# Clustered attention with a top-2 mixture of experts on one core: the gate's products in 16 columns, a changed order around the first expert, less scratch for dynamic transfers

## The chip, the cores and the metric

One Trainium2 chip, one core of it. The metric is the device time of one execution in microseconds (us): the median of 3 runs. The five engines are named as in the profile: PE (matmuls, PEld its weight loads), DVE (vector), ACT (scalar), POOL (GpSimd), SP (the engine whose queue issues most transfers).

## What is computed

The reference, cut to what matters:

```python
# attention: q, k, v of shape (4, 8, 768, 64); 16 centroids for each head
q_assign = argmax(normalized q @ normalized centroids)     # k_assign likewise
mask = q_assign[:, :, :, None] == k_assign[:, :, None, :]
scores = where(mask, q @ k.T / 8, -1e9)
x = softmax(scores) @ v                                    # then (3072, 512): heads side by side
# mixture of experts: 8 experts, 512 -> 1024 -> 512
noisy = x @ w_gate + log1p(exp(x @ w_noise)) * noise
top2 = the two largest of 8;  weight = softmax of the two
out[token] = sum over its two experts of weight * (relu(x @ w1[e]) @ w2[e])
```

## The kernel before, in words

Four batches of 8 heads are worked off as 16 pairs of heads (p = 0 to 15; pairs 0 to 3 are batch 0, and so on). The attention is one list of 192 steps t, six key blocks for each of two heads of a pair; a step's `scores` (4 matmuls of 384 columns, two exponentials on ACT into `pe`), `split_p` of the step before (the low half `pl = pe - high half`, on POOL, for the last 19 steps on DVE) and `values` of the step four before (18 matmuls into `av`). In between stand helpers, put at a step (in thirds of a step) by the table `AT` and the method `at`: each engine gets its instructions in this order and works them off in order. The helpers that matter here:

- `load_qk` (L379): q and k of four heads of a batch, 4 x 768 x 64 floats each, on SP's queue. `a_split` transposes them on PE and writes `hl` (high and low halves, L463 on ACT and L464 on DVE, one buffer). `b_place` (L528) copies `hl` by ten transfers of SP into the score operands A and B. `b_mask` places the cluster masks `mk` into A. `b_max` (L557 on PE, L559 on DVE) finds the row maxima, `b_neg` and `b_negT` (L566 to L575) turn them and place them in B through `nm` and `nt`.
- At the end of a head `values` writes x: `rs` (L628, L629) from `av` and a factor `ch`, then `xt` (L631). `x_scale` makes a batch's factor in seven steps, the last of which, `heads` (L430), makes `ch` on DVE.
- `x_halves` (L667 on ACT, L668 on POOL) splits a pair's 128 columns of x into two f16 halves `xh`; `store_x` stores them, `turn_h` (L1136) transposes them by a transfer of SP into `xhT` (one buffer). `g_logits` (L686 to L695) multiplies them with the gate's weights: for each of 6 token blocks and both halves of x one matmul with 32 columns (high and low halves of 16 weights); DVE scales and adds up over the four pairs of a batch in `glg` (L690, L692), and after the fourth adds the two halves to `gl` (L695). `g_gate` is a chain of some 40 small instructions on DVE and ACT from `gl` to each token's two places in the experts' lists; `g_list` (L847, L848) writes them to a table by indirect transfers of POOL.
- Around the end: `load_list(0)` reads the first expert's list, `gather_x` (L1157, POOL) gathers four tiles of 128 tokens, `turn_x` (L1168, SP) transposes them into `xT`.

`experts` then runs, for the first expert, `layer1` over 8 blocks f of 128 hidden units for the first 512 tokens of its list (12 matmuls of 512 columns in each, then ACT and DVE write `hT`, L1186 and L1187), with w2's conversion (`split_w2`) in between, and the last batch's gate: `g_logits(15)` before block 3 (`ahead=3`), then the chain `fs` cut into pieces before the blocks. `l_hot` and `l_sum` (L821, L838) make the rest of the lists by matmuls, between the first tiles of `layer2`. The other seven experts follow the same way with 404-column matmuls.

Of the kernel before, what the change touches and what calls it, by code (L numbers as in the profile page):

```python
# [9 lines left out]
F32 = mybir.dt.float32  # L10
# [15 lines left out]
AT = dict(  # L26
    ahead=3,
    first={'place': -2.333, 'sims': [-3.333, -2.667], 'sum': [-2.333, -2.333], 'max1': -2.333, 'ge': -2.333, 'max2': -2.333, 'eq': -1.333, 'mask': -1.0, 'bmask': -1.0, 'ky': -2.333, 'split': [-5.333, -5.0, -5.333, -4.0], 'bmax': [3.667, 22.667], 'bstep': [1.0, 0.667], 'neg': [9.0, 26.667], 'negT': [9.333, 27.333]},
    L=4, qk=-20.667, v=-8.667,
    vscale=-0.667, vsplit=10.667, vstep=1.0, split=[-4.667, -3.667, -4.0, -3.333], place=-0.667,  # L30
    sims=[-3.0, 2.0], sum=[2.333, 3.333], max1=3.333, ge=3.667, max2=4.333, eq=4.667, mask=6.333, bmask=6.333,
    bmax=9.333, neg=20.333, negT=22.0, zero=31.0, zstep=12.0, zlist=21.0, v1=4.0, store=2.667, turn=6.667, glog=12.0,
    xh=1.333, xh0=4.0, list=[32.0, 32.0, 19.0], lstep=[2.0, 2.0, 1.1667], bstep=1.0,
    gate=[13.0, 13.0, 5.667], am=5.333, amstep=0.333, xs=6.0, ky=4.0, cut=[13, 20], gplace=[27.0, 27.0, 14.333],
    vd=[1, 1, 2, 3, 4, 5], sec=-6.0, qf=-4.0, place1=4.333,
    fv=[{'v': -5.0, 'vscale': 13.0, 'am': 24.333, 'amstep': 0.333, 'vsplit': 25.333, 'vstep': 2.0},
# [8 lines left out]
class Kernel:  # L45
# [175 lines left out]
    def attention(self, ctx):  # L221
# [17 lines left out]
        self.qk, self.vt, self.vv, self.am, self.xt, self.gx = {}, {}, {}, {}, {}, {}  # L239
        self.vm, self.ch, self.wm0 = {}, {}, {}  # L240
        self.ws = {(0, m): self.gp.tile([128, 2], F32, name=f"ws{m}") for m in (1, 2)}
        L = AT["L"]
# [11 lines left out]
        for p in range(NP):  # L254
            b, hp = divmod(p, H // 2)
            w = 12 * (p - 2)
            if hp == 0:
                for g in range(2):
                    at(w + T["qk"] + 24 * g + (T["qf"] if (b, g) == (0, 1) else 0), self.load_qk, b, g)
                    v = w + 24 * g  # L260
                    V = T["fv"][g] if p == 0 else T
                    at(v + V["v"] + (T["v1"] if (b, g) == (1, 0) else 0), self.load_v, b, g)
                    for h in range(0, 4, 2):
                        at(v + V["vscale"] + V["amstep"] * h, self.v_max, b, g, h)
                    chain(v + V["am"], V["amstep"], self.v_scale(b, g))
                    if g:
                        chain(v + V["xs"] - (4 if b else 0), 1.0 if b else 0.333, self.x_scale(b))
                    for h in range(4):
                        at(v + V["vsplit"] + V["vstep"] * h, self.v_split, b, g, h)
# [30 lines left out]
            if p + 1 < NP:  # L300
                at(z + T["xh"] + (T["xh0"] if p == 0 else 0), self.x_halves, p)
                at(z + T["store"] + (T["xh0"] if p == 0 else 0), self.store_x, p)
                turn, glog = (T["store"], 5.667) if p == NP - H // 2 - 1 else (T["turn"], T["glog"]) if p < NP - 2 else (5.0, 8.0)
                at(z + turn, self.turn_h, p)
                at(z + glog, self.g_logits, p)
            if hp == H // 2 - 1:
# [41 lines left out]
        for t in range(min(sched)[0], z + L + 2):  # L348
            u = t - L
            slot = lambda i: [f(*a) for f, a in sched.pop((t, i), [])]  # L350
            slot(0)
            if 0 <= t < z:
                self.scores(t // 12, (t % 12) // 6, t % 6)
            if 0 <= t - 1 < z:
                self.split_p((t - 1) // 12, ((t - 1) % 12) // 6, (t - 1) % 6)
            slot(1)
            if 0 <= u < z:
                p, s, kc = u // 12, (u % 12) // 6, u % 6
                for i in range(NJ):
                    if AT["vd"][i] == kc:  # L360
                        self.values(p, s, i)
            slot(2)
# [61 lines left out]
    def x_scale(self, b):  # L424
        nc = self.nc

        def heads():
            self.ch[b] = self.wk.tile([128, 8], F32, name="ch")
            for g in range(2):
                nc.vector.tensor_scalar(self.ch[b][:, 4 * g:4 * g + 4], self.am[b, g][:, 2, :], self.xsc[:, b, 0:1], None,  # L430
                                        op0=OP.mult)

        return self.power(self.wk, lambda: self.vm[b], lambda: self.xsc[:, b], 3) + [heads]
# [228 lines left out]
    def x_halves(self, p):  # L662
# [4 lines left out]
        nc.scalar.activation(xh[:, :, 0], x, AF.Copy)  # L667
        nc.gpsimd.tensor_tensor(xh[:, :, 1], x, xh[:, :, 0], op=OP.subtract)  # L668

# [6 lines left out]
    def g_logits(self, p):  # L676

        nc, NJ, E = self.nc, self.NJ, self.E
        b, hp = divmod(p, self.H // 2)
        s = self.wgs[:, 2:3]  # L680
        if hp == 0:
            self.lg = self.gp.tile([128, NJ, 2, 2 * E], F32, name="glg", bufs=1)
        t = self.ps()[:, :NJ * 4 * E].rearrange("p (j i e) -> p j i e", j=NJ, i=2)
        for j in range(NJ):
            for i in range(2):
                nc.tensor.matmul(t[:, j], self.xhT[:, 2 * j + i], self.wgh[:, hp], start=(j == 0 and i == 0),  # L686
                                 stop=bool(i), skip_group_check=True)
        if hp == 0:
            nc.vector.tensor_tensor(s, self.wgs[:, 0:1], self.xsc[:, b, 0:1], op=OP.mult)
            nc.vector.tensor_scalar(self.lg, t, s, None, op0=OP.mult)  # L690
        else:
            nc.vector.scalar_tensor_tensor(self.lg, t, s, self.lg, op0=OP.mult, op1=OP.add)  # L692
        if hp == self.H // 2 - 1:
            self.gl = self.gp.tile([128, NJ, 2 * E], F32, name="gl", bufs=1)
            nc.vector.tensor_tensor(self.gl, self.lg[:, :, 0], self.lg[:, :, 1], op=OP.add)  # L695

    def g_gate(self, b):
# [9 lines left out]
        def begin():  # L707
# [6 lines left out]
            T["p"] = self.aux  # L714
            nc.scalar.activation(w(0), self.gl[:, :, E:], AF.Abs)

# [9 lines left out]
        pt = lambda: T["p"][:, c0:c0 + NE + E]  # L726
        nl = lambda: self.gl[:, :, :E]
        ns = lambda: self.gl[:, :, E:]
        rf = lambda: T["rec"].bitcast(F32)
# [168 lines left out]
    def experts(self, ctx):  # L898
# [36 lines left out]
        self.unscale(0, self.lst0.bitcast(F32)[:, :, 1])  # L935
# [198 lines left out]
    def turn_h(self, p):  # L1134
        self.xhT = self.gp.tile([128, 2 * self.NJ, 128], F16, name="xhT", bufs=1)
        self.nc.sync.dma_start_transpose(self.xhT, self.xh.rearrange("p j i c -> p (j i c)"))  # L1136

# [140 lines left out]
```

## Time and profile before

| | |
|---|---|
| median of 3 runs | 1054.55 us (1050.92 to 1058.95) |
| profiled execution | 1046.11 us; span 1044.3 us |
| mean granted clock of PE over the span | 0.979 |
| PE busy | 976.2 us (93%) |
| DVE, POOL, ACT busy | 683.2, 569.6, 447.0 us |

The profile is of one execution. Busy time is the union of an engine's instructions; a row of a timeline gives start, duration and, in brackets, how long the engine was idle before and what released it.

### The profile page before, as it was taken

How to read it: one execution, taken by the hardware profiler on the slowest of the kernel's cores; microseconds unless marked ns; L12 is line 12 of the kernel's file. 1: busy time of each engine (PE TensorE's matmuls, PEld its weight loads, DVE VectorE, ACT ScalarE, POOL GpSimd, SP SyncE). 2: the span in 40 equal slices, each digit the busy share in tenths (PEclk: the TensorE clock that was granted, in tenths of full speed). 3: DMA queues.
4: the chain of work that ended last, by engine and by line, in shares of the span. 5: the costliest groups of instructions: out<-in, count | busy, mean ns of one | idle time of the engine just before them, and what ended most of it. 6: DMA issues, size and time to landing. Idle time of an engine off the chain costs nothing.

```text
span 1044.3 us, 21670 instructions
## 1 busy us (share of the span) xinstructions
PE 976.2 (93%) x8359; PEld 663.1 (63%) x8359; DVE 683.2 (65%) x1493; ACT 447.0 (43%) x875; POOL 569.6 (55%) x618
## 2 busy tenths in 40 slices
PE   5799899999989998987999999999999999999994
PEld 4578798889888897875455545445454454554541
DVE  5888678887889878895746555464564644646521
ACT  3467576758566767664122313124122241121400
POOL 9269596868997799974355225133251342522211
PEclk8899999999999999998999999999999999999997
DMA  7866888887988776746267565545656456663200
GB/s 202 213 166 140 204 202 220 219 209 172 216 202 213 169 180 139 199 108 149 97 162 224 147 190 173 136 144 149 167 177 159 133 158 152 182 154 131 61 34 35
DMA packets 181902, 169.34 MB, mean 162 GB/s; under 512 B 93159, under 2 KB 159079, under 8 KB 181794
## 3 DMA queue, kind: packets, MB, share of 16 engines
q1 hardware_dynamic: 167990, 131.02, 50.7%
q0 software_dynamic: 13296, 36.38, 11.1%
q8 instruction: 67, 1.10, 0.4%
q10 hardware_dynamic: 508, 0.50, 0.3%
q14 instruction: 41, 0.34, 0.1%
HBM read 81.80 MB, written 26.12 MB: 103 GB/s over the span
## 4 chain that ended last, share of the span: by engine, by line
PE 42%; issue 7%; DVE 2%; POOL 2%; DMA 1%; SPq 0%; ACT 0%; POOLq 0%; DVEq 0%
PE ring L1177 20%; PE ring L1217 19%; POOL out L1230 1%; PE ring L1207 1%; POOL xt L1192 1%; DMA xg<-xs,lst 1%; DVE wm L1101 1%; PE ring L1211 0%; SPq L1168 0%; DMA xhT<-xh 0%; DVE hT L1187 0%; PE ring L838 0%; DVE w2t L1113 0%; DMA out<-yo,idx 0%; PE ring L166 0%
## 5 line engine op out<-in xcount | busy, mean ns | idle before, releaser
L599 POOL TENSOR_TENSOR pl<-pe 128x768 f16<-128x768 f32 x173 | 251.8, 1470 | 58.3 <-ACT pe L588 54.6
L1177 PE MATMUL ring<-xT,w1t 128*128 128x404 f16 (+2 forms) x1536 | 266.9, 334 | 0.0
L1217 PE MATMUL ring<-w2t,hT 128*128 128x512 f16 x1152 | 250.8, 379 | 0.4 <-DVE w2t L1113 0.4
L588 ACT ACTIVATE pe<-ring,l 128x384 f32<-128x384 f32 x384 | 201.4, 577 | 83.2 <-PE ring L587 73.2
L559 DVE TENSOR_REDUCE mm<-ring 128x1 f32<-128x384 f32 x384 | 193.1, 548 | 51.3 <-PE ring L557 50.9
L1177 PEld LDWEIGHTS <-w1t 128*128 128x128 f16 x1536 | 148.0, 97 | 114.9 <-issue 2.5
L1230 POOL DMA_INDIRECT out<-yo,idx x52 | 58.7, 1128 | 285.6 <-DVE yo L1226 207.5
L1217 PEld LDWEIGHTS <-hT 128*128 128x128 f16 x1152 | 112.4, 98 | 135.2 <-issue 1.1
L1186 ACT ACTIVATE hT<-ring 128x404 f16<-128x404 f32 (+3 forms) x128 | 56.6, 487 | 203.1 <-PE ring L1177 203.1
L587 PE MATMUL ring<-B 128*128 128x384 f32 x384 | 130.5, 340 | 1.6 <-DMA B<-nt 1.6
L1187 DVE SCALAR_TENSOR_TENSOR hT<-ring,hT 128x404 f16<-128x404 f32 (+3 forms) x128 | 66.0, 553 | 74.9 <-ACT hT L1186 74.9
L1226 DVE SCALAR_TENSOR_TENSOR yo<-ring,lsw,xt 128x512 f32<-128x512 f32 (+1 forms) x49 | 36.7, 748 | 110.3 <-PE ring L1217 104.3
L587 PE MATMUL ring<-A 128*128 128x384 f32 x264 | 98.7, 374 | 4.3 <-ACT pe L588 3.6
L616 PE MATMUL av<-vv,pe 128*128 128x65 f16 x1152 | 99.1, 196 | 2.9 <-DVE xt L631 2.9
L618 PE MATMUL av<-vv,pe 128*128 128x64 f16 x1152 | 98.3, 194 | 0.0
L616 PEld LDWEIGHTS <-pe 128*128 128x128 bf16 x1152 | 81.9, 100 | 16.5 <-issue 10.2
L1112 ACT ACTIVATE w1t<-stg,ws 128x1024 f16<-128x1024 f32 x32 | 34.4, 1138 | 121.2 <-DVE ws L180 121.2
L557 PE MATMUL ring<-A 128*128 128x384 f32 x264 | 74.9, 357 | 6.9 <-DMA xs<-xh 2.3
L618 PEld LDWEIGHTS <-pe 128*128 128x128 bf16 x1152 | 79.7, 99 | 0.3
L587 PEld LDWEIGHTS ring<-B 128*128 128x128 f32 x384 | 73.4, 191 | 2.3 <-DMA B<-nt 2.3
L622 PE MATMUL av<-vv,pl 128*128 128x65 f16 x1152 | 67.4, 195 | 1.7 <-POOL pl L599 1.3
L1157 POOL DMA_INDIRECT xh<-xs,idx x52 | 56.6, 1089 | 16.5 <-issue 15.6
(211 smaller groups left out, 1340.2 us busy)
## 6 DMA issues: line engine op xcount, KB each, us to landing
stg<-in_moe_w SPq DMA_DIRECT2D x64, 512.0 KB, 4.6
B<-hl SPq DMA_DIRECT2D x30, 384.0 KB, 4.4
A<-hl SPq DMA_DIRECT2D x20, 384.0 KB, 6.7
vt<-in_v SPq DMA_DIRECT2D x8, 768.0 KB, 9.1
out<-zt SPq DMA_DIRECT2D x12, 512.0 KB, 6.6
B<-hl SPq DMA_DIRECT2D x30, 192.0 KB, 4.2
xs<-xh SPq DMA_DIRECT2D x15, 384.0 KB, 3.1
qk<-in_q SPq DMA_DIRECT2D x7, 768.0 KB
```

Of the source, the lines that this page charges most:

```text
L557: nc.tensor.matmul(t, A[:, 0, s, j * 128:j * 128 + 128], A[:, 1, s, n * 384:n * 384 + 384], start=True, stop=True)
L559: nc.vector.tensor_reduce(st["mm"][:, c, n:n + 1], t, axis=X, op=OP.max, negate=True)
L587: nc.tensor.matmul(t, M[:, 1 - qi, s, ks], M[:, qi, s, ns], start=not qi, stop=bool(qi))
L588: nc.scalar.activation(pe[:, n], t, AF.Exp, bias=self.l64[:, 0:1], scale=self.scale)
L599: (nc.vector if last else nc.gpsimd).tensor_tensor(lo, pe, hi, op=OP.subtract)
L616: nc.tensor.matmul(av[:, j, :], ph[:, js], vv[:, hh, kj, 64:129], start=(kc == 0 and j == 0), stop=False, skip_group_check=True)
L618: nc.tensor.matmul(av[:, j, :64], ph[:, js], vv[:, hh, kj, 0:64], start=False, stop=False, skip_group_check=True)
L622: nc.tensor.matmul(av[:, j, :], pl[:, js], vv[:, hh, kj, 64:129], start=False, stop=(kc == NJ - 1), skip_group_check=True)
L1177: nc.tensor.matmul(p, self.w1t[:, wi, c, f * 128:f * 128 + 128], self.xT[:, c, xi, n0:n1], start=(i == 0), stop=(i == 3 * ND - 1))
L1187: nc.vector.scalar_tensor_tensor(h1, x, 0.0, h0, op0=OP.max, op1=OP.subtract)
L1217: nc.tensor.matmul(p, self.hT[:, hi, f, t * 128:t * 128 + 128], self.w2t[:, wi, f], start=(i == 0), stop=(i == 3 * NF - 1))
L1230: i = nc.gpsimd.indirect_dma_start(out=self.out, out_offset=bass.IndirectOffsetOnAxis(ap=en[:r], axis=0), in_=yo[:r], in_offset=None, boun ...
```

## The change

The gate: `g_logits` multiplies with high and low weights separately, 16 columns each, and sums high by high, high by low and low by high in one place, 18 matmuls of 16 columns instead of 12 of 32; the product of the two low halves is left out. `gl` is added up directly over the four pairs; `glg` and the addition at the end are gone.

The order: `load_qk` of batches 1 to 3 stands 7.333 steps later (batch 0's stays); `heads` moves from DVE to POOL and later by up to 1.333 steps; the gate's chains start 0.667 step later, and so does `g_logits(11)`; `split_p` of eight steps near the end (173 to 180) comes up to two steps later than before; `x_halves` of pairs 13 and 14 has its subtraction on DVE; `g_logits(14)` moves from the attention into the first expert, ahead of `g_logits(15)`, and pair 15 has a transposed buffer of its own. The first expert's first layer runs twice over the 8 blocks, on 256 tokens each, instead of once on 512; what stood between its blocks keeps its place.

The scratch for dynamic transfers is 8192 bytes of a partition instead of the 16384 of the default.

```diff
-    ahead=3,
+    ahead=6,
-    L=4, qk=-20.667, v=-8.667,
+    L=4, qk=-13.333, v=-8.667,
-    gate=[13.0, 13.0, 5.667], am=5.333, ...
+    gate=[13.667, 13.667, 6.333], am=5.333, ...
-    vd=[1, 1, 2, 3, 4, 5], sec=-6.0, qf=-4.0, place1=4.333,
+    vd=[1, 1, 2, 3, 4, 5], sec=-6.0, qf=[-7.333, -11.333], place1=4.333,
...
-                        chain(v + V["xs"] - (4 if b else 0), 1.0 if b else 0.333, self.x_scale(b))
+                        fs = self.x_scale(b)
+                        chain(v + V["xs"] - (4 if b else 0), 1.0 if b else 0.333, fs[:-1])
+                        at(v + V["xs"] + (2.667 if b else 3.333), fs[-1])
...
-                turn, glog = (T["store"], 5.667) if p == NP - H // 2 - 1 else ...
+                turn, glog = (T["store"], 6.333) if p == NP - H // 2 - 1 else ...
-                at(z + glog, self.g_logits, p)
+                if p < NP - 2:
+                    at(z + glog, self.g_logits, p)
...
-            if 0 <= t - 1 < z:
-                self.split_p((t - 1) // 12, ((t - 1) % 12) // 6, (t - 1) % 6)
+            for x in range(t - 3, t):
+                if 0 <= x < z and t - x == (1 if x < z - 19 or x > z - 12 else 3 if x < z - 15 else 2):
+                    self.split_p(x // 12, (x % 12) // 6, x % 6)
...
-                nc.vector.tensor_scalar(self.ch[b][:, 4 * g:4 * g + 4], self.am[b, g][:, 2, :], self.xsc[:, b, 0:1], None,
+                nc.gpsimd.tensor_scalar(self.ch[b][:, 4 * g:4 * g + 4], self.am[b, g][:, 2, :], self.xsc[:, b, 0:1], None,
...
-        nc.gpsimd.tensor_tensor(xh[:, :, 1], x, xh[:, :, 0], op=OP.subtract)
+        (nc.vector if self.NP - 4 < p < self.NP - 1 else nc.gpsimd).tensor_tensor(xh[:, :, 1], x, xh[:, :, 0], op=OP.subtract)
...
-        s = self.wgs[:, 2:3]
+        s, xhT = self.wgs[:, 2:3], self.xhT.pop(p)
         if hp == 0:
-            self.lg = self.gp.tile([128, NJ, 2, 2 * E], F32, name="glg", bufs=1)
-        t = self.ps()[:, :NJ * 4 * E].rearrange("p (j i e) -> p j i e", j=NJ, i=2)
+            self.gl = self.gp.tile([128, NJ, 2 * E], F32, name="gl", bufs=2)
+        t = self.ps()[:, :NJ * 2 * E].rearrange("p (j e) -> p j e", j=NJ)
         for j in range(NJ):
-            for i in range(2):
-                nc.tensor.matmul(t[:, j], self.xhT[:, 2 * j + i], self.wgh[:, hp], start=(j == 0 and i == 0),
-                                 stop=bool(i), skip_group_check=True)
+            for i, (xi, wi) in enumerate(((0, 0), (0, 1), (1, 0))):
+                nc.tensor.matmul(t[:, j], xhT[:, 2 * j + xi], self.wgh[:, hp, wi], start=(j == 0 and i == 0),
+                                 stop=(i == 2), skip_group_check=True)
         if hp == 0:
-            nc.vector.tensor_tensor(s, self.wgs[:, 0:1], self.xsc[:, b, 0:1], op=OP.mult)
-            nc.vector.tensor_scalar(self.lg, t, s, None, op0=OP.mult)
+            nc.vector.tensor_scalar(s, self.wgs[:, 0:1], self.xsc[:, b, 0:1], None, op0=OP.mult)
+            nc.vector.tensor_scalar(self.gl, t, s, None, op0=OP.mult)
         else:
-            nc.vector.scalar_tensor_tensor(self.lg, t, s, self.lg, op0=OP.mult, op1=OP.add)
-        if hp == self.H // 2 - 1:
-            self.gl = self.gp.tile([128, NJ, 2 * E], F32, name="gl", bufs=1)
-            nc.vector.tensor_tensor(self.gl, self.lg[:, :, 0], self.lg[:, :, 1], op=OP.add)
+            nc.vector.scalar_tensor_tensor(self.gl, t, s, self.gl, op0=OP.mult, op1=OP.add)
...
-        for f in range(NF):
+        n = TA * 64
+        for f in range(2 * NF):
             i = f - AT["ahead"]
             if i == 0:
+                self.g_logits(p - 1)
                 self.g_logits(p)
-            if i >= 0:
-                for x in fs[cut[i]:cut[i + 1]]:
+            if i >= 0 and i % 2 == 0:
+                for x in fs[cut[i // 2]:cut[i // 2 + 1]]:
                     x()
-            self.layer1(0, f, [A])
-            if f < 3 or f == 7:
-                self.split_w2(0, min(f, 3))
-                self.load_w1(1, min(f, 3))
+            self.layer1(0, f % NF, [(n * (f // NF), n * (f // NF) + n)])
+            if f in (1, 3, 5, 15):
+                self.split_w2(0, min(f // 2, 3))
+                self.load_w1(1, min(f // 2, 3))
...
-    nc = bacc.Bacc("TRN2", target_bir_lowering=False, num_devices=1)
+    nc = bacc.Bacc("TRN2", target_bir_lowering=False, num_devices=1, dynamic_dma_scratch_size=8192)
```

## Rows read from the trace of the kernel before

**Rows 1.** Page, part 1: busy us (share of the span) xinstructions.
```profile
PE 976.2 (93%) x8359; PEld 663.1 (63%) x8359; DVE 683.2 (65%) x1493; ACT 447.0 (43%) x875; POOL 569.6 (55%) x618
```
**Rows 2.** PE's waits by releaser: us in total, times, longest us.
```profile
PE ring L686 <- DMA xhT<-xh: 7.1, 2, 5.7
```
**Rows 3.** Windows: us, busy of each engine, PEclk, DMA share, GB/s.
```profile
121.00:131.00 10.00, 7.67 (x80) 6.77 (x78) 4.97 (x12) 5.52 (x12) 3.39 (x4) 0.83 0.68 159
305.00:315.00 10.00, 7.67 (x89) 7.20 (x85) 9.80 (x21) 6.40 (x14) 7.72 (x6) 0.83 0.60 174
```
**Rows 4.** Timeline of PE, end of attention: start, us, instruction, count, idle before.
```profile
475.66 0.34 PE L622 MATMUL av<-vv,pl 128*128 128x65 f16 x6
476.20 0.34 PE L622 MATMUL av<-vv,pl 128*128 128x65 f16 x6
482.23 0.50 PE L686 MATMUL ring<-wgh,xhT 128*128 128x32 f16 x12 [5.68 <-DMA xhT<-xh]
...
486.10 1.24 PE L1177 MATMUL ring<-xT,w1t 128*128 128x512 f16 x5
```
**Rows 5.** Timeline of SP's queue there (issue times).
```profile
478.47 1.47 SPq L1136 DMA_TRANSPOSE xhT<-xh  x1
```
**Rows 6.** Timelines of DVE, POOL and PE in batch 1's gate.
```profile
304.03 3.17 DVE L695 TENSOR_TENSOR gl<-glg 128x96 f32<-128x96 f32 x1
...
301.35 5.73 POOL L599 TENSOR_TENSOR pl<-pe 128x768 f16<-128x768 f32 x4
...
308.00 0.59 PE L587 MATMUL ring<-A 128*128 128x384 f32 x1 [2.33 <-ACT pe L588]
```
**Rows 7.** Timelines of DVE and PE around 285 us.
```profile
283.15 3.81 DVE L430 TENSOR_SCALAR ch<-am,xsc 128x4 f32<-128x4 f32 x2
...
287.46 0.44 PE L475 MATMUL ring<-hl,wh 128*128 128x384 f32 x1 [1.61 <-DVE hl L464]
```
**Rows 8.** Timelines of SP's queue and PE around 120 us.
```profile
112.88 1.45 SPq L379 DMA_DIRECT2D qk<-in_q  x1
...
115.55 1.31 SPq L528 DMA_DIRECT2D A<-mk  x2
...
124.15 0.66 PE L557 MATMUL ring<-A 128*128 128x384 f32 x1 [2.33 <-DMA xs<-xh]
```
**Rows 9.** Timeline of PE at one g_logits, and the next instruction.
```profile
463.09 0.45 PE L686 MATMUL ring<-wgh,xhT 128*128 128x32 f16 x12
463.39 0.42 PE L587 MATMUL ring<-A 128*128 128x384 f32 x1
```
**Rows 10.** Chain of waits, first expert's layer 1: start, us, what.
```profile
486.26 7.78 PE ring L1177 x36
...
535.71 10.57 PE ring L1177 x84
```
**Rows 11.** Timelines of DVE and POOL at the last batch's first rs.
```profile
400.76 0.22 DVE L628 TENSOR_SCALAR rs<-av,ch 128x6 f32<-128x6 f32 x1
...
400.90 2.89 POOL L599 TENSOR_TENSOR pl<-pe 128x768 f16<-128x768 f32 x2
```
**Rows 12.** Timelines of DVE and PE around 450 us.
```profile
447.75 3.94 DVE L599 TENSOR_TENSOR pl<-pe 128x768 f16<-128x768 f32 x1
...
453.31 0.33 PE L573 MATMUL ring<-ident,nm 128*128 128x128 f32 x1 [1.51 <-DVE nm L568]
```
**Rows 13.** SP's queue and ACT at one b_place; two windows (columns of rows 3).
```profile
192.37 2.59 SPq L528 DMA_DIRECT2D B<-hl  x2
...
199.84 0.49 ACT L463 ACTIVATE hl<-ring 128x384 fp32r<-128x384 f32 x1
...
66.00:68.00 2.00, 2.00 (x14) 1.69 (x13) 1.90 (x8) 1.58 (x4) 1.03 (x1) 1.00 0.92 339
133.00:135.00 2.00, 2.00 (x25) 2.00 (x22) 0.77 (x2) 1.97 (x5) 2.00 (x3) 1.00 0.89 190
```
**Rows 14.** Groups by line and form, DVE, first expert: busy us, mean ns, idle.
```profile
L1187 DVE SCALAR_TENSOR_TENSOR hT<-ring,hT 128x512 f16<-128x512 f32 x8 | 5.4, 685 | 2.7 <-ACT hT L1186 2.7
```

More of the change, by code (lines that the diff above doesn't have):

```diff
@@ L33 @@
     xh=1.333, xh0=4.0, list=[32.0, 32.0, 19.0], lstep=[2.0, 2.0, 1.1667], bstep=1.0,
-    gate=[13.0, 13.0, 5.667], am=5.333, amstep=0.333, xs=6.0, ky=4.0, cut=[13, 20], gplace=[27.0, 27.0, 14.333],
-    vd=[1, 1, 2, 3, 4, 5], sec=-6.0, qf=-4.0, place1=4.333,
+    gate=[13.667, 13.667, 6.333], am=5.333, amstep=0.333, xs=6.0, ky=4.0, cut=[13, 20], gplace=[27.0, 27.0, 14.333],
+    vd=[1, 1, 2, 3, 4, 5], sec=-6.0, qf=[-7.333, -11.333], place1=4.333,
     fv=[{'v': -5.0, 'vscale': 13.0, 'am': 24.333, 'amstep': 0.333, 'vsplit': 25.333, 'vstep': 2.0},
@@ L239, in attention @@
         self.qk, self.vt, self.vv, self.am, self.xt, self.gx = {}, {}, {}, {}, {}, {}
-        self.vm, self.ch, self.wm0 = {}, {}, {}
+        self.vm, self.ch, self.wm0, self.xhT = {}, {}, {}, {}
         self.ws = {(0, m): self.gp.tile([128, 2], F32, name=f"ws{m}") for m in (1, 2)}
@@ L258, in attention @@
                 for g in range(2):
-                    at(w + T["qk"] + 24 * g + (T["qf"] if (b, g) == (0, 1) else 0), self.load_qk, b, g)
+                    at(w + T["qk"] + 24 * g + (0 if b else T["qf"][g]), self.load_qk, b, g)
                     v = w + 24 * g
@@ L302, in attention @@
                 at(z + T["store"] + (T["xh0"] if p == 0 else 0), self.store_x, p)
[L303 removed]
+                turn, glog = (T["store"], 6.333) if p == NP - H // 2 - 1 else (T["turn"], T["glog"]) if p < NP - 2 else (5.0, 8.0)
                 at(z + turn, self.turn_h, p)
[L305 removed]
+                if p < NP - 2:
+                    at(z + glog, self.g_logits, p)
             if hp == H // 2 - 1:
@@ L714, in begin @@
             T["p"] = self.aux
-            nc.scalar.activation(w(0), self.gl[:, :, E:], AF.Abs)
+            T["gl"] = self.gl
+            nc.scalar.activation(w(0), ns(), AF.Abs)
         w = lambda i: T["w"][:, i]
@@ L726, in g_gate @@
         pt = lambda: T["p"][:, c0:c0 + NE + E]
-        nl = lambda: self.gl[:, :, :E]
-        ns = lambda: self.gl[:, :, E:]
+        nl = lambda: T["gl"][:, :, :E]
+        ns = lambda: T["gl"][:, :, E:]
         rf = lambda: T["rec"].bitcast(F32)
@@ L1134, in turn_h @@
     def turn_h(self, p):
-        self.xhT = self.gp.tile([128, 2 * self.NJ, 128], F16, name="xhT", bufs=1)
-        self.nc.sync.dma_start_transpose(self.xhT, self.xh.rearrange("p j i c -> p (j i c)"))
+        self.xhT[p] = (self.gp if p + 1 < self.NP else self.mo).tile([128, 2 * self.NJ, 128], F16, name="xhT" if p + 1 < self.NP else "xlT", bufs=1)
+        self.nc.sync.dma_start_transpose(self.xhT[p], self.xh.rearrange("p j i c -> p (j i c)"))
     def open_x(self):
```

## The prediction

> **What bounds the kernel now.** First the page's first part: PE is busy 976.2 of 1044.3 us and no other engine more than 65% [rows 1]. So the time is PE's work plus the 68 us in which it waits, and an edit on another engine counts only where it ends a wait of PE. Second, PE's waits by releaser [rows 2], and windows around the long ones: a wait over 2 us is followed by a lower mean granted clock, 0.83 over ten us twice [rows 3] (the two levels are 2.4 and 1.2 GHz), so it is paid a second time, 0.17 x 10 = 1.7 us of full-speed work. Third, the timelines of the other engines inside those waits, to name what came last there. Behind the first expert the chain of waits is PE's own work almost to the end, and the diff touches nothing there. The change can act in attention, in the passage into the first expert, and in that expert's first stretch.
>
> **The passage.** After its values at 476.5 PE idles 5.68 us for the g_logits of pair 14 [rows 4]: SP issues the transposed halves they read at 478.47, behind the four expert transposes [rows 5]. The change takes this g_logits out of PE's order here and puts it behind six half blocks of layer 1, when that transpose has long landed. Four groups of values stand behind the wait; they take about 3.5 of the 3.87 us from 482.23 to 486.10, and at the 0.54 that one takes before the wait (475.66 to 476.20 [rows 4]) they would take 2.2: 1.3 to 1.4 us of low clock go with the wait. What is late next? On DVE one pl and the last w1t split stood behind the glg of the same g_logits; freed, they run while PE does its four groups. The last xT transposes are issued until 478.4, just when layer 1 would start at 478.7; a pass over 512 columns would wait for them to land, some 3 us. The pass over the first 256 doesn't read them. Gain 5.7 + 1.4 = **7.1**; ends 4 (layer 1 waits those 3 us after all) and 7.1.
>
> **gl summed in 16 columns.** The separate addition that makes gl goes. In batch 1 DVE stood 3.17 us on it, until POOL's run of four pl ended (301.35 + 5.73); ACT waited for gl with exponentials queued behind, PE idled 2.33 us [rows 6] and then ran at the 0.83. Gain 2.3 + 1.7 = **4.0**; ends 0 (the stall moves to another instruction) and 4.0. On PE 12 matmuls become 18, sixteen times. Twelve of 32 columns take from 463.09 to 463.39 [rows 9], 25 ns each. No row shows 16 columns: if the pace falls with the columns, 18 take 0.23 us, 0.07 less than now; if 25 is a floor, 0.45, 0.15 more. A group of values, 18 matmuls of 64 or 65 columns, takes 0.54 [rows 4], 30 ns each: twice the columns cost a fifth more, so I take the floor, 16 x 0.15 = **+2.4**; ends -1.2 and +2.4.
> The Trainium skill, "TensorE: Matmul & The Clock Gate", section "Wait — 56ns, not 53.3ns?", speaks against this edit: start to start never falls below about 25 ns, however few the columns. By that rule the sum has +2.4, by columns -1.2; the 25 ns of the row agree with the rule.
>
> **ch on POOL.** Two DVE instructions of 128x4 go, once 3.81 us long; PE lost 1.61 behind them [rows 7]. Gain **1.6**; ends 0 and 1.6. But ch now comes behind a pl in POOL's order. In the last batch DVE wants it for its rs at 400.76, while POOL's pair of pl runs from 400.90 [rows 11]; the first ends at 402.4, ch at about 402.8. DVE stands 2 us, the evacuation of av behind it, and PE wants av for the next head. The g_logits of pair 11 also moves 0.667 slot later there, which by itself would end the shorter of the two waits of rows 2 (7.1 - 5.7 = 1.4). I let PE wait 2.2 in place of 1.4: **+0.8**; ends -1.4 and +2.2.
>
> **q and k loaded later.** At 112.88 SP issues q (k follows) just ahead of the masks at 115.55; PE then waits 2.33 us for the tile that the masks complete [rows 8], and 0.83 follows [rows 3]. The load leaves this place: gain **4.0**; ends 0 (the placements were late by themselves) and 4.0. Its new place is right ahead of b_place, six times. The next hl may be written only when b_place has read the old one. At a tight one the last placements are issued until 194.96 and ACT writes hl at 199.84 [rows 13]: 4.9 us, in which they must also land; I take half, 2.5, as spare. The load is 1.5 MB (two times 4 heads of 768 x 64 x 4 bytes): 4.5 us at the 339 GB/s of the stretch with a v load, 7.5 at the 190 of a stretch with placements [rows 13]. At 4.5 the tight one waits 2.0 us, of which about 0.8 don't reach PE (in rows 6 DVE stood 3.17 and PE 2.33): 1.2. I take **+1.5** for all six, ends 0 and 35 (below).
>
> **split_p later, two x_halves on DVE.** Around 450 one pl takes DVE 3.94 us, while POOL runs a pl and x_halves of pair 13; the last maxima and nm queue behind it, and PE waits 1.51 for nm [rows 12]. The change holds four pl on DVE back by two steps and four by one, past POOL's last pl, and puts x_halves of pair 13 into their place. DVE's work is about even, nm earlier: gain **1.5**; ends -3 (x_halves takes the 3.94) and 3.2 (1.5 and a stretch of low clock). That of pair 14 adds its time to DVE where DVE is only just ahead, and takes away a POOL instruction that DVE's pl there could meet: 0, end +3.
> The Trainium skill, "SBUF — State Buffer", section "Who interferes with whom": a DVE instruction with two SBUF inputs and a GpSimd one that reads SBUF exclude each other for a whole instruction. This speaks for taking the gl addition away and against x_halves on DVE, which reads two SBUF tiles; the 3.17 and 3.94 us agree. By the rule the two x_halves cost up to 6 us where the sum has 0.
>
> **First expert.** 192 matmuls of 256 columns for 96 of 512. 84 of 296 take 10.57 us (126 ns), 36 of 512 take 7.78 (216) [rows 10]; on that line one of 256 takes 109, so 20.95 for 20.75: **+0.2**, ends 0 and 3.4 (126 each). DVE gets sixteen hT where it had eight at 0.685 us [rows 14], in between the last batch's gate, whose chain on DVE ends this stretch. Halves cost between 0.34 and 0.685 each, so 0 to 5.5 in all; no row separates an instruction's fixed part, and I take a quarter of the way, 1.4, with two thirds of it inside the chain: **+0.9**.
>
> **Scratch of 8 KB.** No row shows POOL waiting for room for its transfers. Zero; the upper end is in the rivals.
>
> **Sum.** Gains 7.1 + 4.0 + 1.6 + 4.0 + 1.5 = 18.2; costs 2.4 + 0.8 + 1.5 + 0.2 + 0.9 = 5.8; net **-12.4**. The profiled execution took 1046.1 us, 1.8 more than its span: 1033.7 for one like it. The runs' median, 1054.55, is 8.4 above; I take the sum from the median: **1042 us**.
>
> **Rivals.**
> *Attention's waits come back.* POOL's pl run back to back [rows 6, 11]; PE, freed of one wait, meets another. Against it: PE's long waits are for single instructions, not for pl as a rule. Then only the passage and the costs count: -7.1 + 2.4 + 0.8 + 0.2 + 0.9 = -2.8, 1052 us. Chance 0.20.
> *Slower: q and k in front of the placements.* At 7.5 us a load and 2.5 spare, hl waits 5.0, PE 4.2, and 1.7 of clock: 5.9 each, six times 35 in place of 1.5: 1076 us. It is slower by over 1% from five such loads. For it: placements moved 190 GB/s with the DMA engines 0.89 busy. Against: 339 with a v load [rows 13]. Chance 0.08.
> *x_halves locks DVE* (what the SBUF page rules). 3.0 us more each by the 3.94, and one stretch of low clock: +7.7, 1050 us. Against: by then POOL has only transfers to issue. Chance 0.08.
> *The scratch binds, or the passage is eaten by a wait for freed memory.* Layer 1 then starts 4 us or more later: 1046 to 1052. No row for it. Chance 0.06.
> *The forecast*: 0.58. Its own range 1031 to 1048: -23 with matmuls by columns (-3.6), the clock at 450 (-1.7), and pair 11 ending its wait (-2.2) and others; +6 with the low end of the passage and of the masks.
>
> **Numbers.** 1% is 10.5 us, about what a measurement of this kernel can tell from no change: faster is under 1044.0, slower over 1065.1. Of the forecast's 0.58, 0.49 lies under 1044, and of the rivals that end at 1046 to 1052 another 0.03: faster 0.52. Slower 0.10: its rival and a little. The rest 0.38. The range, 1031 to 1054, takes in the rivals at 1050 and 1052; out of it are the slower one and the tails.
>
> **What would show it.** Passage: no wait of PE for xhT between the last scores and layer 1, whose first matmul comes some 2.2 us later at full clock. gl: no DVE instruction of the gate over 0.5 us. Gate matmuls: 18 in 0.45 us. q and k: PE's wait at the masks gone; ACT or DVE waiting to write hl would prove the slower rival. ch: DVE waiting for POOL at the first rs of the last batch. The forecast is wrong if PE's waits before the passage are not at least 5 us less in all.

## The result, and the profile after

The changed kernel takes 1041.92 us (median of 4 runs, 1039.12 to 1044.49) where the kernel before takes 1052.98 (4 runs); the ratio is 0.9884 (95% interval 0.9846 to 0.9921), 12.2 us of 1053; the medians are 11.1 us apart. The prediction said 1042, and faster. The sum came out; four of its terms did not, and they cancelled, which is luck. The prediction also named a sign by which its forecast would be wrong; that sign came, though the time was right.

The profiled execution of after took 1042.58 us. The kernel before's profiled execution, 1046.11, had been faster than all its timed runs (1050.92 to 1058.95); between the two profiles lie only 3.5 us. Taking the sum from the median was the right choice: from the profiled execution it would have been 1033.7. In two other profiled executions of the same attention (the kernel before again, and with less scratch, both below, on a slower chip) the first scores begin 2 us later than its 41.33 us, and from the first to the last of them it takes 436 us, not 432.4.

The page of after, part 1, answers to [rows 1] (busy us, share of the span, instructions):

```profile
PE 978.9 (94%) x8551; PEld 678.0 (65%) x8551; DVE 668.8 (64%) x1491; ACT 448.4 (43%) x883; POOL 564.4 (54%) x624
```

Timeline of PE in after, from the last scores into the first expert; answers to [rows 4]:

```profile
481.89 0.34 PE L591 MATMUL ring<-B 128*128 128x384 f32 x1
...
486.59 8.08 PE L1181 MATMUL ring<-xT,w1t 128*128 128x256 f16 x72 [0.52 <-DMA xT<-xg]
494.51 0.60 PE L690 MATMUL ring<-wgh,xhT 128*128 128x16 f16 x18
494.96 0.60 PE L690 MATMUL ring<-wgh,xlT 128*128 128x16 f16 x18
495.42 10.64 PE L1181 MATMUL ring<-xT,w1t 128*128 128x256 f16 x96
```

The last scores (L587 before, at 473.69 us) now come at 481.89, 8.2 us later; layer 1 starts at 486.59 instead of 486.10. So the passage gave 7.7 us, and what stands ahead of it lost them: 3.0 us before the first scores (44.37 us against the 41.33, which is the earliest of all profiles), 5.2 from the first to the last. The largest new group in PE's waits (us in total, times, longest us) is this; before has one such wait, of 0.5 us:

```profile
PE ring L458 <- DVE hl L468: 10.6, 6, 2.3
```

The sign of a wrong forecast was that PE's waits before the passage are not at least 5 us less. Windows from the start to the last scores, before and then after (us, busy of each engine, PE first, then the granted clock, DMA share, GB/s):

```profile
0.00:473.69 473.69, 429.75 (x5359) 384.27 (x5359) 386.50 (x966) 310.23 (x614) 375.73 (x336) 0.97 0.78 187
```
```profile
0.00:481.89 481.89, 433.10 (x5442) 390.80 (x5443) 373.36 (x959) 311.00 (x614) 372.86 (x342) 0.98 0.78 185
```

PE is idle for 43.9 us before and 48.8 after: 4.9 more, not 5 less. (In the two kernels of the section on the gathers, which have q and k at their old places, it is 42.9 and 41.9.)

Here is one of the six waits for hl. Timelines of after, of SP's queue (issue times), ACT and PE; they answer to [rows 13]:

```profile
184.61 1.55 SPq L1140 DMA_TRANSPOSE xhT<-xh  x1
186.21 0.98 SPq L383 DMA_DIRECT2D qk<-in_q  x1
187.25 1.04 SPq L383 DMA_DIRECT2D qk<-in_k  x1
188.39 2.08 SPq L532 DMA_DIRECT2D A<-hl  x3
190.57 1.96 SPq L532 DMA_DIRECT2D B<-hl  x2
192.62 5.40 SPq L532 DMA_DIRECT2D A<-hl  x3
198.12 2.77 SPq L532 DMA_DIRECT2D B<-hl  x2
...
206.39 0.87 ACT L467 ACTIVATE hl<-ring 128x384 fp32r<-128x384 f32 x2 [2.67 <-DMA wst<-in_moe_w]
...
207.53 0.78 PE L458 MATMUL ring<-ident,qk 128*128 128x128 f32 x3 [2.10 <-DVE hl L468]
```

Read it from below. PE's transpose waits 2.10 us for a DVE instruction that follows ACT's hl; ACT may write hl only when b_place has read the old one. The last of those transfers is issued at 200.9, 5.9 us later than before. Some 4.1 of these are that the whole stretch stands later (xhT's transfer, issued at 184.61, was issued at 180.49); 2.2 are q and k, which now go in between. ACT stands idle for 2.67 us and writes at 206.39 where it wrote at 199.84: 5.5 us after the end of the last issue. The releaser that the row on ACT names, a transfer of wst, doesn't write or read hl; it is taken here for the one that only came last.

The program's end moved too. POOL's instructions at the program's last line and at the branch around `extra`, before and then after (duration ns min/median/max, first and last start):

```profile
L1274 POOLq DRAIN  x3: 46/107/7016, 1036.4 to 1044.0; - x3
L1036 POOLq INC_SWDGE_SEM  x1: 1890/1890/1890, 1034.5 to 1034.5; - x1
```
```profile
L1278 POOLq DRAIN  x3: 46/107/3177, 1036.8 to 1040.5; - x3
L1040 POOLq INC_SWDGE_SEM  x1: 948/948/948, 1035.8 to 1035.8; - x1
```

No engine is busy behind the last output, so 0.94 + 3.84 = 4.8 us of the gain are POOL's closing instructions, which are not counted as busy and have no line of the page. The 3.5 us between the two profiles are then 7.7 of the passage and 4.8 of the end, less 8.2 ahead of the passage and 0.8 in the first expert.

### The profile page after: what moved, and what is told of

Its sections match the earlier page's. It is cut to its first block, busy times and chain, and to the rows that moved or that the text cites. A ratio compares the mean times of both kernels' runs of the same rounds, so it can differ in the third digit from the quotient of the medians.

```text
span 1040.8 us, 22073 instructions
## 1 busy us (share of the span) xinstructions
PE 978.9 (94%) x8551; PEld 678.0 (65%) x8551; DVE 668.8 (64%) x1491; ACT 448.4 (43%) x883; POOL 564.4 (54%) x624
## 4 chain that ended last, share of the span: by engine, by line
PE 66%; DVE 10%; issue 8%; POOL 6%; DMA 6%; ACT 4%; ACTq 0%; SPq 0%; POOLq 0%; DVEq 0%
PE ring L1181 20%; PE ring L1221 19%; PE ring L591 7%; PE ring L561 4%; DVE mm L563 3%; ACT pe L592 2%; PE av L620 2%; PE av L626 2%; PE av L622 2%; PE ring L479 2%; DMA B<-hl 2%; PE aux L494 2%; PE ring L458 1%; DMA wst<-in_moe_w 1%; POOL out L1234 1%
## 5 line engine op out<-in xcount | busy, mean ns | idle before, releaser
L1181 PEld LDWEIGHTS <-w1t 128*128 128x128 f16 x1632 | 157.4, 97 | 107.1 <-issue 2.5
L1190 ACT ACTIVATE hT<-ring 128x404 f16<-128x404 f32 (+2 forms) x136 | 57.4, 469 | 201.2 <-PE ring L1181 201.2
L1191 DVE SCALAR_TENSOR_TENSOR hT<-ring,hT 128x404 f16<-128x404 f32 (+2 forms) x136 | 66.6, 529 | 74.3 <-ACT hT L1190 74.3
L620 PEld LDWEIGHTS <-pe 128*128 128x128 bf16 x1152 | 81.1, 100 | 15.5 <-issue 11.3
L1105 DVE TENSOR_REDUCE wm<-stg 128x1 f32<-128x1024 f32 x56 | 65.5, 1207 | 0.0
```

Source lines behind the costliest of these rows:

```text
L620: nc.tensor.matmul(av[:, j, :], ph[:, js], vv[:, hh, kj, 64:129], start=(kc == 0 and j == 0), stop=False, skip_group_check=True)
L1181: nc.tensor.matmul(p, self.w1t[:, wi, c, f * 128:f * 128 + 128], self.xT[:, c, xi, n0:n1], start=(i == 0), stop=(i == 3 * ND - 1))
L1191: nc.vector.scalar_tensor_tensor(h1, x, 0.0, h0, op0=OP.max, op1=OP.subtract)
```

## The experiments

Kernels whose results are compared by their ratios stand beside runs of the kernel before on the same chip. On two of the chips the kernel before takes 1094 to 1095 us, on the others 1052 to 1053; the section on the slower chips says where those 42 us are. Times from the last scores to layer 1 are from start to start, read from PE's timeline.

### The kernel before once more, and with 8 KB of scratch alone

The first is the kernel before without an edit; the second:

```diff
-    nc = bacc.Bacc("TRN2", target_bir_lowering=False, num_devices=1)
+    nc = bacc.Bacc("TRN2", target_bir_lowering=False, num_devices=1, dynamic_dma_scratch_size=8192)
```

> The kernel before once more, for a second profile of it. Theory A (what the two profiles show is the programs' own): layer 1 of the first expert starts at about 486 us, POOL's last instructions (the release of the transfer scratch and its last drain) take 1.9 and 7.0 us again, PE waits 5 to 6 us for xhT before the last values. Theory B (the pair of profiles differs by scatter of single executions): layer 1 starts 5 or more us away from 486, or the last drain takes 3 to 4 us.

> The kernel before with 8 KB of scratch and nothing else changed. Theory A: the last drain of POOL falls from 7.0 to about 3.2 us and the release ahead of it from 1.9 to 0.95, all else stays: 4.8 us faster, ratio 0.9954. Theory B: the drain's length is scatter, ratio 1.000. The prediction's rival (the scratch binds): POOL waits at its indirect transfers, ratio over 1.003.

Measured, on a slower chip: 1094.39 us the kernel before (11 runs), 1082.57 with 8 KB, ratio 0.9898 (0.9868 to 0.9927), so 11.2 us. POOL's end took 0.95 and 3.18 us against 1.89 and 7.02: 4.8 us again. The other 6.4 us are not at the end, and the passage is not shorter (11.6 and 13.1 us from the last scores to layer 1). Layer 1 started at 491.5 and 492.4 us, more than 5 later than the 486: in that, theory B of the first expectation holds (on another chip than the first profile's), and A for POOL's end. PE's wait for xhT was 4.5 and 6.0 us: the 5.68 of [rows 4] is one draw.

### The changed kernel with 16 KB

The same line, undone in the changed kernel.

> The changed kernel once more, beside the other three on one chip, as the point from which each of them is read. If the gain comes from the passage and from the end of the program, as the two profiles say, its ratio to the kernel before is 0.988 as in the first result, within 0.004, and the profile shows a wait of PE at L458 for hl of about 10 us in all. If the gain hangs on where PE's instructions come from, the ratio differs by more than 0.005.

> The changed kernel with the scratch of 16384 bytes again. Theory S (the scratch is only cleared at the end of the program): all stages up to the last output as in the changed kernel; POOL's last instructions take 1.9 and 7.0 us again in place of 0.95 and 3.2; ratio to the kernel before 0.0046 higher than the changed kernel's (4.8 us). Rival S2, that the scratch also acts while the kernel runs: 0.008 to 0.012 higher, with the difference in the stages of the experts. The prediction had 0.

Measured, on the other slower chip: the changed kernel 0.9857 (0.9834 to 0.9880), with 16 KB 0.9964 (0.9943 to 0.9985). The difference is 0.0107, 11.7 us with some 3.4 to either side. The passage agrees (4.28 and 4.29 us), and POOL's end takes 1.89 and 7.02 us again. So S holds for 4.8 us. S2 is right that the times have more, but its place isn't shown: in the two profiles the experts take the same time (520.2 and 520.6 us from the first to the last, as measured in the section on the slower chips). That the changed kernel's ratio is 0.9857 here and was 0.9884 fits both.

### q and k at their old places

```diff
-    L=4, qk=-13.333, v=-8.667,
+    L=4, qk=-20.667, v=-8.667,
...
-    vd=[1, 1, 2, 3, 4, 5], sec=-6.0, qf=[-7.333, -11.333], place1=4.333,
+    vd=[1, 1, 2, 3, 4, 5], sec=-6.0, qf=[0.0, -4.0], place1=4.333,
```

> The changed kernel with q and k loaded where they were (qk=-20.667, qf 0 and -4). Theory A (the moved loads delay the placements, and the write of hl waits for these): the six waits of PE for hl (10.6 us in the changed kernel's profile) are gone, layer 1 of the first expert starts 6 to 9 us earlier than there, the time is 5 to 9 us below the changed kernel's: ratio to before 0.980 to 0.984. Theory C (as predicted, the move is a gain of 2.5 us): 2 to 3 us slower than the changed kernel, with the wait of 2.3 us at the masks back: ratio about 0.991.

Measured: 1072.23 us, ratio 0.9799 (0.9772 to 0.9825): undoing this part makes the changed kernel faster, 0.0058 below the 0.9857 that it has on the other slower chip, 6.4 us with 3.8 to either side. From the first to the last scores it takes 432.1 us here. On the one chip of the section above it is 432.0 with the old places (the run with 4 KB below) and 438.2 and 440.0 with the new. The wait for hl in PE's waits, and the wait for the masks' tile in PE's timeline:

```profile
PE ring L458 <- DVE hl L468: 0.5, 1, 0.5
```
```profile
125.04 0.60 PE L561 MATMUL ring<-A 128*128 128x384 f32 x2 [1.44 <-DMA xs<-xh]
```

The wait of [rows 8] is back, as the prediction had it (there 2.33; 1.4 to 2.5 in all nine profiles with the old places, none in the five with the new), but it is one wait, and it was traded for five. The 0.5 for hl that is left is in before too.

### q and k moved, alone

The kernel before with that table's new values.

> The kernel before with one part of the change alone: load_qk at its new places. Theory A (the load stands in SP's queue ahead of b_place, so hl is freed late): PE waits at L454 for hl some 8 to 11 us in all, the last scores come 4 to 8 us later than in the kernel before, ratio 1.004 to 1.008. Theory B, that of the prediction: the wait at the masks goes (4.0) and 1.5 comes, ratio 0.998, and no wait for hl over 1.5 us.

Measured: ratio 1.0030 (1.0007 to 1.0052), 3.3 us slower. PE's waits:

```profile
PE ring L454 <- DVE hl L464: 6.4, 4, 2.5
```

Theory A holds in sign and mechanism; the price is just below its lower end, with three waits for hl over 1 us where the changed kernel has five. Which of the change's other parts makes hl wanted earlier wasn't told apart.

### g_logits(14) back in the attention

```diff
-                if p < NP - 2:
-                    at(z + glog, self.g_logits, p)
+                at(z + glog, self.g_logits, p)
...
-                self.g_logits(p - 1)
                 self.g_logits(p)
```

> The changed kernel with the g_logits of pair 14 back in the attention, 8 steps behind the end of its values as before; two passes of layer 1 kept. Theory A (the passage is worth 7 us): PE waits again 4 to 6 us for xhT of pair 14 before the last values, with a stretch of low clock behind: 5 to 7.5 us slower than the changed kernel, ratio to before 0.994 to 0.997. Rival: the wait is gone anyway because x_halves of pair 14 on DVE brings its transposed halves earlier: within 2 us of the changed kernel, ratio 0.988 to 0.990.

Measured: ratio 0.9926 (0.9897 to 0.9954), 9.32 us from the last scores to layer 1 against 4.29 in the changed kernel: 5.0 us. At the place of [rows 4] PE waits 2.9 us for xhT again (theory A had 4 to 6, and its ratio begins at 0.994), and the granted clock over the nine us there is 0.82, the low level (1.2 GHz) for part of them. Most of the passage's gain is this move's.

### The scratch of 4 KB

The changed kernel with q and k at their old places, and

```diff
-    ..., dynamic_dma_scratch_size=8192)
+    ..., dynamic_dma_scratch_size=4096)
```

> The changed kernel with load_qk at its old places and a scratch of 4096 bytes. If POOL's end goes with the scratch, its last two instructions take about 0.5 and 1.3 to 1.6 us, and the kernel ends 2.0 to 2.4 us earlier than with the old places alone: ratio to the kernel before 0.977 to 0.978 if that one is at 0.980 again. Rival: POOL waits for room at the four gathers, layer 1 starts 2 us or more later than in that kernel and the gain is gone.

Measured, POOL's end:

```profile
L1278 POOLq DRAIN  x3: 46/107/1381, 1072.8 to 1074.7; - x3
L1040 POOLq INC_SWDGE_SEM  x1: 508/508/508, 1072.3 to 1072.3; - x1
```

It goes with the scratch: 8.91, 4.13 and 1.89 us for 16, 8 and 4 KB, some 0.6 us for each KB. Layer 1 starts 4.01 us after the last scores: nothing waits for room at the gathers. But the ratio was 0.9876 (0.9853 to 0.9899), 0.008 above that of 8 KB on the other slower chip: no gain here, a miss.

### The gate's 16 columns alone

The kernel before with `g_logits` of the changed kernel (18 matmuls, gl summed directly).

> The kernel before with the gate's products in 16 columns alone (gl summed directly, no addition of halves). The prediction's terms: 18 matmuls of g_logits take 0.45 us from the first to the next line's first, and PE's wait of 2.33 us behind DVE's addition is gone; 4.0 less and 2.4 more, 1.6 us net, ratio 0.9985. Rival: another instruction of DVE stands behind POOL's pl instead, the wait comes back under another line, ratio 1.002.

Measured, on a chip where the kernel before takes 1052.34 us: 1046.27, ratio 0.9955 (0.9930 to 0.9979): 4.7 us (2.2 to 7.4). Timeline of PE:

```profile
111.25 0.60 PE L686 MATMUL ring<-wgh,xhT 128*128 128x16 f16 x18
111.70 0.42 PE L587 MATMUL ring<-xT 128*128 128x384 f32 x1
```

18 matmuls in 0.45 us, the number predicted. PE has no wait between 300 and 316 us, where [rows 6] had 2.33, and the next ones (0.36 and 0.75, by 327) are for mm: none of that size came in its place there. In all, PE is idle for 23.6 us from the first to the last scores, 26.6 in before. The passage was 15.5 us in this profile, 12.4 in before's, so the two profiles don't show the gain; the times do.

### ch, split_p and x_halves undone

The changed kernel with q and k at their old places, and

```diff
-                if 0 <= x < z and t - x == (1 if x < z - 19 or x > z - 12 else 3 if x < z - 15 else 2):
+                if 0 <= x < z and t - x == 1:
...
-        (nc.vector if self.NP - 4 < p < self.NP - 1 else nc.gpsimd).tensor_tensor(xh[:, :, 1], ...
+        nc.gpsimd.tensor_tensor(xh[:, :, 1], ...
...
-                nc.gpsimd.tensor_scalar(self.ch[b][:, 4 * g:4 * g + 4], ...
+                nc.vector.tensor_scalar(self.ch[b][:, 4 * g:4 * g + 4], ...
```

with `heads` back in the chain of `x_scale`.

> The changed kernel with load_qk at its old places and three more parts undone: ch on DVE and at its old place, split_p one step after its scores everywhere, x_halves of pairs 13 and 14 on POOL. The prediction priced these three at 2.3 us net (1.6 - 0.8 + 1.5): the last scores 2.3 us later than with them (474.3), PE waits again 1.5 us for nm near step 180 and about 1.6 for hl near the end of batch 0; ratio 0.002 higher than with them. Rival: they are worth nothing, the waits only change their line, last scores within 1 us of 474.

Measured: 1034.69 us, ratio 0.9838 (0.9815 to 0.9860), against 0.9810 with the three parts (next section): 2.9 us, with 3.7 to either side, so the times alone don't tell the theories apart. Nor do the last scores: they come at 472.3 us, between the 476.9 and 470.7 of the two kernels with the parts. Timeline of PE without the three parts, then with them:

```profile
447.69 0.35 PE L624 MATMUL av<-vv,pl 128*128 128x65 f16 x6 [1.32 <-POOL pl L601]
451.68 0.33 PE L575 MATMUL ring<-ident,nm 128*128 128x128 f32 x1 [1.50 <-DVE nm L570]
453.57 0.21 PE L618 MATMUL av<-vv,pe 128*128 128x65 f16 x1 [0.85 <-DVE xt L633]
```
```profile
454.45 0.35 PE L626 MATMUL av<-vv,pl 128*128 128x65 f16 x6 [0.81 <-POOL spacer L849]
460.10 0.44 PE L591 MATMUL ring<-B 128*128 128x384 f32 x1 [0.99 <-DMA B<-nt]
```

The wait for nm of [rows 12] is back in the first and gone in the second, and with it low clock (windows of ten us about the wait; the column after the engines is the granted clock):

```profile
446.00:456.00 10.00, 6.33 (x87) 5.21 (x84) 9.83 (x15) 4.77 (x9) 8.93 (x13) 0.89 0.54 113
```
```profile
452.00:462.00 10.00, 8.20 (x122) 7.12 (x117) 8.38 (x17) 6.35 (x13) 8.69 (x14) 1.00 0.44 100
```

The last 24 steps of attention take 41.8 us without the parts (41.6 and 41.7 in before and with the gate's columns alone) and 39.35 with them, in after and in both kernels of the next section: 2.4 us.

### The experts' gathers one by one

The changed kernel with q and k at their old places, and in the experts, in the second kernel with 16 KB,

```diff
-            if e + 1 < E:
-                for t in range(T):
-                    self.gather_x(e + 1, t)
             for f in range(NF):
                 self.layer1(e, f, [(0, n), (n, CAP)])
+                if f < T and e + 1 < E:
+                    nc.gpsimd.tensor_copy(self.spacer, self.hT[0:1, 1, f, n:n + 1])
+                    self.gather_x(e + 1, f)
```

> load_qk at its old places, and from the second expert on POOL's seven gathers of the next expert one after each block of layer 1 (POOL copies one number of that block's hT first) instead of thirteen transfers in a row. Theory G (on some chips PE's stalls in the experts, 1.4 us for each of about five matmuls while it waits for nothing that the profile shows, belong to these bursts of POOL): from the second expert's first layer on no such stall, 67.2 us from expert to expert instead of 73 to 76; ratio to the kernel before 0.945 to 0.955 where that one shows seven stalls, 0.980 where it shows none. Rival: the stalls stay in their places or move with the gathers, ratio 0.975 to 0.985.

> The same with the scratch of 16384 bytes. If the 11 us that the scratch made on two chips are 4.8 at POOL's end and one stall of PE more in the experts, and the spread gathers take the stalls away, then what is left of it is the 4.8: ratio 0.0045 higher than with 8192 bytes. If the scratch acts in another way while the kernel runs: 0.010 higher, as before. If it acted only at the end all along: 0.0045 with stalls too.

On the chip of these two no kernel shows a stall of PE in the experts: 67.23 us from expert to expert in all four kernels there, in bursts or spread. So they don't test theory G; what they do say: 1033.00 us, ratio 0.9810 (0.9783 to 0.9838) with 8 KB, 1035.48, ratio 0.9838 (0.9816 to 0.9861) with 16. Spreading costs nothing that the profiles show. The scratch is 2.9 us here with 3.8 to either side: 4.8 is inside, 11 is not. And q and k at their old places are worth 0.9884 - 0.9810, 7.8 us with 4.9 to either side, on chips without stalls (two chips, and with the gathers spread in one of the two kernels). The one with 8 KB has the shortest time of the study; it has all of the change but the move of q and k, and the spread gathers besides. The 0.9799 of the kernel without these, on a slower chip, can't be told from its 0.9810.

## The slower chips

Where the kernel before takes 1094 us, PE stalls in layer 1 of the experts, from the second on. Timeline of PE in the kernel before there, and POOL's at the same time:

```profile
589.02 0.50 PE L1177 MATMUL ring<-xT,w1t 128*128 128x404 f16 x2 [1.10 <-issue]
590.42 0.49 PE L1177 MATMUL ring<-xT,w1t 128*128 128x404 f16 x1 [0.89 <-issue]
591.85 0.50 PE L1177 MATMUL ring<-xT,w1t 128*128 128x404 f16 x1 [0.94 <-issue]
```
```profile
587.04 0.99 POOL L1157 DMA_INDIRECT xh<-xs,idx  x1 [0.30 <-issue]
588.34 1.00 POOL L1157 DMA_INDIRECT xh<-xs,idx  x1 [0.30 <-issue]
589.64 0.93 POOL L1157 DMA_INDIRECT xh<-xs,idx  x1 [0.30 <-issue]
```

"issue" means that PE waited for nothing that the profile shows. Four to six matmuls come about 1.4 us apart, and behind them the granted clock is low (0.68 from 592 to 600 us): 2 to 8 us for each stall, mostly 5.5 or more, one for nearly each expert, always at the end of POOL's run of indirect transfers or just behind it. Such runs are there on the other chips too, without a stall, so they alone don't make one. In the first expert's second layer PE waits in their place 2.1 to 2.7 us for hE of DVE, and that is counted as a stall below. From the first to the last expert (from PE's first matmul on hE in the one, 546.12 us in before, to that in the other) the chips without stalls take 480.8 us, these 514 to 528.

The scratch may have a part in their number. The three profiles with 16 KB show seven, those with 8 KB five, six, six and six, the one with 4 KB seven; one stall more, about 7 us, would be what 11.2 and 11.7 have over the 4.8, and what the 4 KB lost. That is an observation on eight profiles, and one pair speaks against it: the changed kernel's six stalls took as long as the seven with 16 KB (520.2 and 520.6 us). What the stalls wait for, and how the scratch would come into it, stays open. No run of the spread gathers is from such a chip.

## Why the prediction came out, point by point

| part | predicted | measured, us | from |
|---|---|---|---|
| gate's 16 columns | -1.6 | -4.7 (-7.4 to -2.2) | the part alone |
| passage and first expert | -6.0 | -6.9 | the two profiles |
| scratch | 0 | -4.8 | POOL's end, all profiles |
| ch, split_p, x_halves | -2.3 | -2.9, 3.7 to either side | undone in the fastest kernel |
| q and k later | -2.5 | +7.8, 4.9 to either side | undone |
| sum | -12.4 | -11.5 | the result: -12.2 |

With intervals of 2.6 to 4.9 us on three of the rows, and parts measured on different chips, it proves little that the measured sum agrees with the result too. For q and k the table has the largest of three figures: 7.8, 6.4, and 3.3 for the move alone.

- **The passage**: right, and for the reason given. PE no longer waits for xhT, layer 1 starts 4.7 us after the last scores instead of 12.4, 7.7 against 7.1; it waits 0.52 us for the gathered rows, not 3, since the first pass needs half of them. The step's input, the 5.68 us, is 4.5 to 8.6 in the four other kernels with before's passage.
- **The first expert**: 60.84 us for 60.02 from layer 1's first matmul to layer 2's first on hE, +0.8 against +1.1. 96 matmuls of 256 columns take 10.64 us, 111 ns each; the 109 was right and the upper end of 126 wrong. The halves of hT take 418 ns (0.685 us for a whole one in [rows 14]), 0.15 more for each pair, about the quarter of the way that was taken. The trace of before had this price: "no row separates an instruction's fixed part" was wrong. By form, DVE in before, behind the row of [rows 14]:

```profile
L1187 DVE SCALAR_TENSOR_TENSOR hT<-ring,hT 128x256 f16<-128x256 f32 x8 | 3.4, 423 | 4.2 <-ACT hT L1186 4.2
```

- **gl**: the mechanism and the cost of 18 matmuls were right. The gain was undersized: 4.7 net by the runs where 1.6 stood; its interval begins at 2.2, and no single wait shows the rest. "No row shows 16 columns" was wrong as well. Timeline of PE in before, twelve matmuls of 48 to 8 columns, two of each, and the next row:

```profile
505.34 0.44 PE L764 MATMUL aux<-goh,ones 128*128 128x48 bf16 x12
505.64 1.24 PE L1177 MATMUL ring<-xT,w1t 128*128 128x512 f16 x5
```

  They take 0.30 us, 25 ns each (bf16 here, f16 in the gate), so the end "by columns" could have been struck out.
- **ch on POOL**: the wait is there and smaller than 1.6 us. With ch still on DVE (2.85 us long in the kernel with the parts undone) PE's wait behind it is this:

```profile
289.81 0.44 PE L477 MATMUL ring<-hl,wh 128*128 128x384 f32 x1 [0.69 <-DVE hl L466]
```

  The 1.61 of [rows 7] was 0.78, 0.62, 0.88 and nothing in the four other executions of the kernel before's order. With ch on POOL no profile has this wait over 0.4 us. The cost that the prediction named is there, and stays on DVE. Timelines of POOL and DVE in the fastest kernel, at the last batch's first rs:

```profile
407.97 0.56 POOL L434 TENSOR_SCALAR ch<-am,xsc 128x4 f32<-128x4 f32 x2
...
408.30 0.23 DVE L632 TENSOR_SCALAR rs<-av,ch 128x6 f32<-128x6 f32 x1 [2.08 <-PE ring L561]
```

  DVE stands 2.08 us (its releaser is again not the one named: rs starts 0.04 us after the end of the first ch), as long as predicted, and no wait of PE over 0.52 us follows in the next 8 us.
- **split_p and x_halves**: right: the wait for nm goes, and the last 24 steps are 2.4 us shorter where 1.5 stood; the low clock behind the wait goes with it, and part of a wait for pl (1.32, then 0.81). x_halves on DVE takes 0.95 us both times, so that rival fell. On the slower chips this stretch is longer, 44 to 45 us, not shorter: there PE has stalls of up to 2.4 us in it that wait for nothing shown.
- **q and k later: the step that failed.** Its first half was right: the masks' wait goes. The second took one place of six as tight and half of the 4.9 us of [rows 13] as spare, +1.5 for all six. Five of the six are tight: PE waits 1.5 to 2.35 us each, 10.1 in all, some seven times the 1.5 that the sum had, before the clock (7.6 to 8.4 in the three other profiles with the new places and the rest of the change). The sixth, of 0.54, is in before too. The slower rival was this mechanism; its price per wait (4.2 us) was too high and its chance too low. Both came from one place standing for all: the spare was read at a single b_place, by half of a difference, where six such places were in the trace to be read. And there was hardly any spare to halve, as far as issues and writes tell: at the five places of after, ACT, held up, writes hl 5.5 to 7.2 us after the end of the last placement's issue; in before it was 4.9 to 6.6 at four of them and 9.9 at one. In [rows 13]'s place q and k put 2.2 us into the queue ahead of the placements, and PE waited 2.1. The load's time was misreckoned a little besides: 1.57 MB take 4.6 us at 339 GB/s and 8.3 at 190, where 4.5 and 7.5 stood.
- **The scratch: a term that was missing.** "No row shows POOL waiting for room" was true, and the later runs confirm it (layer 1 starts as early with 4 KB). The step failed by asking only what the scratch does while the kernel runs. The 8.9 us of POOL's closing instructions lay in the trace of before, behind the last output, and no term of the prediction's sum goes beyond the first expert.
  The Trainium skill, "VectorE: DVE Perf Modes", section "The DRAIN you can't avoid", puts the DRAINs at a program's ends at some 12 ns whatever the kernel. DVE's two here are 10 and 17 ns and agree; POOL's 7016, 3177 and 1381 don't. By the page the DRAINs would have been alike at every size of the scratch.

So, by the table, the total was right because a term that was 10 us too low met a missing 4.8, a gate term 3.1 too small and a passage 0.9 too small. That is luck: without the scratch, which the sum put at nothing, the changed kernel would have been 7.4 us faster by the result, not 12.4. In the attention alone the rival "attention's waits come back" (0.20) was nearer than the forecast: PE waits more there than before, for hl and not for what the change took away.

## What to carry to other kernels

Read the span behind the last output too: what an engine still does there is in the trace, and a size that nobody waits for while the kernel runs may set how long that takes. Before moving a load in a queue, go through what stands behind it at every place it lands, and ask of each what buffer it frees; read the spare there from the rows, place by place. One shorter wait is easily traded for five. And undo the parts of a change one at a time even when the sum came out: here that gave a kernel some 8 us faster than the changed one by the two ratios, with 4.9 to either side. And hold the sum's total and the signs that were named with it apart: here the one was right and the other wrong.

## What the runs showed of the hardware

- POOL's closing instructions go with the scratch for dynamic transfers: 1.89 + 7.02 us at 16 KB, 0.95 + 3.18 at 8, 0.51 + 1.38 at 4, the same to 0.01 us in all profiles of a size.
- Chips differ by 42 us of 1053 on the same program, 33 to 47 us of it in the experts, where on the slower ones PE has stalls in which it waits for nothing that the profile shows, at the end of POOL's runs of up to thirteen indirect transfers.
- Waits read from one profiled execution are draws: before's passage wait was 5.68 us, and 4.5, 6.0, 6.0 and 8.6 in the four other profiles with the same passage.
